# Half slots of an expert kernel: three instead of two of the four second-weight chunks in high and low parts

## Chip, core and metric

The kernel runs on one core of a Trainium2 chip. The metric is the device time of one execution in microseconds (us), lower being better. TensorE is called PE, VectorE DVE, ScalarE ACT, GpSimd POOL and SyncE (which issues the weight loads) SP, as in the profile.

## The reference

Three parts run one after the other: attention over 32 memories, a Fourier mixing with a dense feed-forward layer, and a routed expert layer. The change touches only the last one. Cut to what matters:

```
x: (4, 576, 512)   w_gate: (512, 8)   w1: (8, 512, 1024)   w2: (8, 1024, 512)
logits = x @ w_gate
for each token: e = its expert (argmax of its logits, or the expert of the token before it)
    p = softmax(logits)
    h = relu(x[b, s] @ w1[e])
    out[b, s] = p[e] * (h @ w2[e])
```

## The kernel before

**Slots.** The tokens of one expert are gathered in slots of up to 256. A slot loads eight weight chunks of 128x1024 fp32 (512 KB each): chunks 0 to 3 hold the expert's first weights, chunks 4 to 7 the second ones. Slots 0 and 1 are written out beside the end of the dense layer; slots 2 to 16 stand one after the other, each under a test on the number of slots, and each in two arms. The first arm is for a full slot. The second arm is for a half slot, one with at most 128 tokens (`narrow`, `turn` and `short_out`). In the profiled execution twelve slots run, and the half arm is taken in slots 3, 4 and 11, which the text calls A, B and C.

**Precision.** A product of fp32 quality is made in one of two ways. Either both factors are split in a high and a low part (type fp32r) and three fast matmuls are added (`products`, L1103 to L1105): high times high, high times low, low times high. Or both factors stay raw fp32 and one slow matmul is issued (L1253), which the trace records as two. Splitting a weight chunk is called a cut: ACT writes the high part (L1327) and DVE or POOL subtracts it from the raw chunk for the low part (L1329). In a half arm the low part of chunk 1 is made on POOL, those of the others on DVE.

**A half slot.** `narrow` makes the hidden values, 128 tokens by 256 for each of the first-weight chunks c = 0 to 3 (tile `pl`). `turn` applies the relu (L1173 on ACT, L1175 on DVE; tile `un`), transposes the result on PE (L1180), and brings it back from PSUM: for c below `SPLIT` as high part on ACT (L1192) and low part on DVE (L1194), for the others as one raw copy (L1185 on ACT or L1187 on DVE). `short_out` multiplies it by second-weight chunk 4 + c, two matmul steps for each c, and then ACT scales the sum (L1261) and POOL writes it out (L1266). The lines that read `SPLIT`:

```
1181            if c >= SPLIT:
1246                w = "cut" if c < SPLIT else "raw", j, 4 + c
1255            if c >= SPLIT and j + 1 < NS:
1448                     ("cut", "late")[arm]: [cuts(*[(j, c) for c in range(4, (8, 4 + SPLIT)[arm])]), cuts(*[(j + 1, c) for c in range(4)])]})
```

The last of these lines also shows that a slot's arm cuts chunks 0 to 3 of the next slot. Line 1255 reloads a chunk that was used raw after its last matmul; a chunk that is cut is reloaded after its cut.

**Order.** `weave` is a planner. Every task yields an engine, a length and what it depends on; the planner picks the step that can start first by its own estimates (`SLOTS`, `SLOT_PACE`) and writes the program in that order. On the chip every engine then runs its own instructions in the written order, and waits at the first one whose inputs are missing. SP does so too, with the weight loads.

Of the kernel before, what the change touches and what calls it, by code (L numbers as in the profile page):

```python
# [84 lines left out]
SLOT_PACE = {"T": 0.928, "V": 0.999, "S": 0.996, "G": 0.946, "D": 1.033}  # L85
LANES = 2
EARLY = 2
SPLIT = 2

FIELDS = ((("ident", 128), ("mask", 4), ("half", 1), ("big", 2)),  # L90
          (("s0", 18), ("tid", 18), ("desc", 8), ("iotaC", 256), ("ohR", 8), ("kR", 1), ("ones", 8), ("k256", 9),
# [86 lines left out]
def attention_fourier_experts_kernel(ctx, tc, qT, phi, kv, w1, w2, wg, wgc, wm, cs, cd, c1, c2, midx, out):  # L178
# [41 lines left out]
    def ended(*names):  # L220
        return [end.get(n, 0.0) for n in names]
# [879 lines left out]
    def products(ps, a, b, first, last):  # L1101

        T.matmul(ps, a[0], b[0], start=first, stop=False)  # L1103
        T.matmul(ps, a[0], b[1], start=False, stop=False)  # L1104
        T.matmul(ps, a[1], b[0], start=False, stop=last)  # L1105
# [58 lines left out]
    def turn(j):  # L1164
        for c in range(4):
# [13 lines left out]
            for x in range(2):  # L1179
                T.transpose(pt[:, 128 * x:128 * x + 128], hr[:, 128 * x:128 * x + 128], id_)  # L1180
            if c >= SPLIT:
                r = yield "SV", {"S": 0.35, "V": 0.42}, [r]
# [55 lines left out]
    def short_out(j):  # L1238
# [4 lines left out]
        for c in range(4):  # L1243
            for x in range(2):
                n = FFN + 8 * j + 2 * c + x
                w = "cut" if c < SPLIT else "raw", j, 4 + c
                yield lambda: ("hid", n) in end and w in end and ("yr", i - 3) in end
                r = yield "T", 0.69 if c < SPLIT else 0.86, ended(("hid", n), w, ("yr", i - 3))
                ts, q = slice(128 * x, 128 * x + 128), slice(512 * x, 512 * x + 512)
                if c < SPLIT:  # L1250
                    products(ps, (hid[n][0][:, ts], hid[n][1][:, ts]), (WH[4 + c][:, q], WL[4 + c][:, q]), c + x == 0, False)
                else:
                    T.matmul(ps, hid[n][:, ts], RAW[4 + c][:, q], start=False, stop=(c + x == 4))  # L1253
                end["used", j, 0, 2 * c + x] = r
            if c >= SPLIT and j + 1 < NS:
                end["raw", j + 1, 4 + c] = yield "D", 1.46, [r]
# [107 lines left out]
    def cuts(*jc):  # L1364
        for j, c in jc:
            yield lambda: j >= NS or all(x in end for x in used(j - 1, c))
            yield from cut(j, c)

    def gather(j):

        yield lambda: ("idx", min(j, 2)) in end and (j == 0 or ("x", NG + j - (2 if j > 2 else 1)) in end)
        yield lambda: j == 0 or ("land", j - 1, 1) in end
        x = gathered[j] = (gathered[j - 2] if j > 3 else
                           stg.tile([128, 1040], F32, name="stg").rearrange("p (t c) -> p t c", t=2))
        for h in range(2):
            end["land", j, h] = yield "G", 1.04, ended(("idx", min(j, 2)), ("ys", NG - 2 if j < 2 else NG - 1))
            G.indirect_dma_start(out=x[:, h], out_offset=None, in_=ys, in_offset=IO(ap=idx[:, h, j:j + 1], axis=0),
                                 bounds_check=N, oob_is_err=False)

    def tokens(j):  # L1380

        if j >= NS:
            return
        k = (NG + j) % 2
        if j < 3:
            yield from gather(j)
        yield lambda: ("land", j, 1) in end
        x = gathered[j]
        before = "first", (16 * NG - 17 if j == 0 else FFN - 1 if j == 1 else FFN + 8 * j - 9)
        yield lambda: before in end  # L1390
        for h in range(2):
            pt, r = yield from turned4(lambda kk: x[:, h, 128 * kk:128 * kk + 128], end["land", j, h] + (5.2 if j < 2 else 3.5))
            hs = slice(128 * h, 128 * h + 128)
            r = yield "S", 0.5, [r] + ended(before)
            S.copy(XH[k][:, :, hs], pt)
            r = yield "V", 0.62, [r]
            V.tensor_tensor(out=XL[k][:, :, hs], in0=pt, in1=f32(XH[k][:, :, hs]), op=ALU.subtract)
            free_pt(r)
            yield lambda: j < 2 or ("yr", 2 * (NG + j) - 3) in end
            yield "V", 0.07, []  # L1400
            j8 = sm_.tile([128, 8], F32, name="j8s")
            V.scalar_tensor_tensor(out=j8, in0=x[:, h, 512:520], scalar=1.0, in1=ohs[:, j] if j > 1 else ohP[:, j], op0=ALU.mult,
                                   op1=ALU.mult, accum_out=PV[k][:, h:h + 1])
        end["x", NG + j] = r
# [18 lines left out]
    with ExitStack() as es:  # L1423
        for j in range(2, NS):
# [13 lines left out]
            for arm in range(2):  # L1438
                with (cmp.Else() if arm else tc.If(half > 0, label=f"half{j}")) as cmp:  # L1439
                    if j + 1 in halves_of:  # L1440
                        tc.mark_branch_hint_location(f"half{j + 1}", halves_of[j + 1], [ET.PE])
                    if FIRST <= j + 1 < NS:
# [4 lines left out]
                    weave({**own, ("tokens", "rows")[arm]: [tokens(j + 1)], "ahead": [gather(j + 2)] if j + 2 < NS else [],  # L1447
                           ("cut", "late")[arm]: [cuts(*[(j, c) for c in range(4, (8, 4 + SPLIT)[arm])]), cuts(*[(j + 1, c) for c in range(4)])]})
                after = before if arm == 0 else full
# [31 lines left out]
```

## Time and profile before

| what | value |
|---|---|
| timed runs | 832.75, 836.06 and 835.94 us, median 835.94 us |
| the profiled execution | 832.19 us, of which the profile's span is 830.4 us |
| PE busy | 802.5 us, 97% of the span |
| DVE, ACT, POOL busy | 546.9, 307.1, 173.7 us |
| mean granted PE clock | 0.993 of full speed |

All times of instructions below are in us from the start of the span. An engine's instructions overlap a little (the next one starts before the end of the last), so what one costs in a row of its kind is the distance between starts. The matmuls' ends are modelled.

### The profile page before, as it was taken

Reading aid. Unit: us, or ns where it says so; the run is one execution under the profiler, and the core shown is the slowest. Engines: PE = TensorE matmul, PEld = TensorE weight load, DVE = VectorE, ACT = ScalarE, POOL = GpSimd, SP = SyncE. Lnnn points to the kernel's source line nnn. Section 1 sums busy time; section 2 is a strip of 40 time slices with the busy share of each in tenths; the row PEclk is TensorE's granted clock in tenths of the full one; section 3 lists DMA queues with packets and bytes.
Section 4 is the critical chain, followed back from the end, with each engine's and each line's share of the span. In section 5 each row is a group of like instructions: output and inputs, shape, how many; then the busy total and the mean of one; then the engine's idle time right before and its main releaser. Section 6 shows DMA issues by size and latency. Waiting matters only on the chain. (4 is left out here: it accounts for less than half of the span.)

```text
span 830.4 us, 14734 instructions
## 1 busy us (share of the span) xinstructions
PE 802.5 (97%) x5500; PEld 697.4 (84%) x5500; DVE 546.9 (66%) x1339; ACT 307.1 (37%) x590; POOL 173.7 (21%) x166
## 2 busy tenths in 40 slices
PE   7999999999999999999999999999999998999993
PEld 6676678888989989889998989889899886899881
DVE  2587766776476876868584766667786565765661
ACT  3465644765111111111111111144464445554441
POOL 0466553553000000000000000020222224121231
PEclk9999999999999999999999999999999999999997
DMA  9877345651310001010000000291786668866563
GB/s 350 339 253 284 117 133 178 218 178 52 130 37 27 26 26 30 24 52 1 27 26 26 26 27 1 83 348 54 258 278 225 208 205 325 301 219 248 199 212 131
DMA packets 35688, 122.09 MB, mean 147 GB/s; under 512 B 5204, under 2 KB 5460, under 8 KB 33802
## 3 DMA queue, kind: packets, MB, share of 16 engines
q1 hardware_dynamic: 30474, 103.76, 36.1%
q0 software_dynamic: 4688, 14.53, 5.1%
q10 hardware_dynamic: 432, 2.60, 0.9%
q8 instruction: 53, 0.87, 0.4%
q14 instruction: 41, 0.34, 0.1%
HBM read 106.10 MB, written 15.56 MB: 147 GB/s over the span
## 5 line engine op out<-in xcount | busy, mean ns | idle before, releaser
L1105 PE MATMUL pl<-xh,w1l 128*128 128x256 f32 x864 | 241.2, 279 | 0.0
L1105 PEld LDWEIGHTS pl<-xh,w1l 128*128 128x128 f32 x864 | 162.3, 188 | 0.0
L1103 PE MATMUL pl<-xh,w1h 128*128 128x256 f32 x576 | 162.3, 282 | 0.0
L1104 PE MATMUL pl<-xl,w1h 128*128 128x256 f32 x576 | 160.9, 279 | 0.0
L1144 ACT ACTIVATE hh<-pl 128x256 fp32r<-128x256 f32 x144 | 55.2, 384 | 281.5 <-PE pl L1105 266.9
L1329 DVE TENSOR_TENSOR w1l<-w1h,w2h 128x1024 fp32r<-128x1024 f32 x91 | 111.7, 1241 | 18.7 <-ACT w2h L1327 12.1
L1327 ACT CAST w2h<-w1h 128x1024 fp32r<-128x1024 f32 x94 | 96.9, 1047 | 49.6 <-issue 34.0
L1103 PEld LDWEIGHTS pl<-xh,w1h 128*128 128x128 f32 x576 | 108.2, 188 | 2.8
L1104 PEld LDWEIGHTS pl<-xl,w1h 128*128 128x128 f32 x576 | 108.1, 188 | 2.4
L1103 PE MATMUL y<-w2h,hh 128*128 128x512 f32 x272 | 108.9, 401 | 0.0
L1105 PE MATMUL y<-w2h,hl 128*128 128x512 f32 x272 | 106.9, 393 | 1.6 <-DVE hl L1146 1.6
L1104 PE MATMUL y<-w2l,hh 128*128 128x512 f32 x272 | 106.7, 392 | 0.5 <-POOL w2l L746 0.5
L840 DVE SCALAR_TENSOR_TENSOR jk<-stg,wgt 128x512 bf16<-128x512 f32 x144 | 99.0, 687 | 4.1 <-DMA wgt<-in_wg_dram 1.6
L1146 DVE SCALAR_TENSOR_TENSOR hl<-pl,hh 128x256 fp32r<-128x256 f32 x144 | 60.4, 421 | 56.1 <-ACT hh L1144 55.5
L1103 PE MATMUL pl<-xh,w2h 128*128 128x256 f32 x288 | 82.6, 287 | 0.0
L1104 PE MATMUL pl<-xl,w2h 128*128 128x256 f32 x288 | 80.8, 281 | 0.0
L349 POOL TENSOR_TENSOR rv<-rv,C 128x1 f32<-128x1 f32 x18 | 12.9, 715 | 269.9 <-DVE rv L347 258.3
L1105 PEld LDWEIGHTS y<-w2h,hl 128*128 128x128 f32 x272 | 51.1, 188 | 13.7 <-DVE hl L1146 2.4
L1103 PE MATMUL y<-w2h,w2l 128*128 128x512 f32 x156 | 62.4, 400 | 0.0
L1105 PE MATMUL y<-w2h,w2l 128*128 128x512 f32 x156 | 61.6, 395 | 0.0
L1104 PE MATMUL y<-w1l,w2l 128*128 128x512 f32 x156 | 61.4, 394 | 0.0
L1104 PEld LDWEIGHTS y<-w2l,hh 128*128 128x128 f32 x272 | 51.2, 188 | 8.9 <-POOL w2l L746 0.8
(249 smaller groups left out, 1350.6 us busy)
## 6 DMA issues: line engine op xcount, KB each, us to landing
w1h<-in_wm_dram SPq DMA_DIRECT2D x104, 512.0 KB
stg<-in_w_dram SPq DMA_DIRECT2D x21, 512.0 KB
kvt<-in_kv_dram SPq DMA_DIRECT2D x8, 1290.0 KB
wgt<-in_w_dram SPq DMA_DIRECT2D x11, 512.0 KB
ys<-stg SPq DMA_DIRECT2D x9, 520.0 KB
qt<-in_qT_dram SPq DMA_DIRECT2D x4, 1156.0 KB
ph<-in_phi_dram SPq DMA_DIRECT2D x8, 288.0 KB
u<-ut SPq DMA_DIRECT2D x12, 192.0 KB
```

What stands on the lines that cost most here:

```text
L349: G.tensor_tensor(out=rv, in0=rv, in1=c_("half"), op=ALU.pow)
L840: V.scalar_tensor_tensor(out=jk, in0=yt[:, t, 0:512], scalar=1.0, in1=wgt[:, e], op0=ALU.mult, op1=ALU.mult, accum_out=L[:, t, e:e + 1])
L1103: T.matmul(ps, a[0], b[0], start=first, stop=False)
L1104: T.matmul(ps, a[0], b[1], start=False, stop=False)
L1105: T.matmul(ps, a[1], b[0], start=False, stop=last)
L1144: S.activation(out=hh, in_=ps, func=AF.Relu)
L1146: V.scalar_tensor_tensor(out=hl, in0=ps, scalar=0.0, in1=f32(hh), op0=ALU.max, op1=ALU.subtract)
L1327: S.copy(WH[c], RAW[c])
L1329: E[mark["eng"]].tensor_tensor(out=WL[c], in0=RAW[c], in1=f32(WH[c]), op=ALU.subtract)
```

## The change

The constant `SPLIT` goes from 2 to 3. In every half arm, chunk 6 is therefore cut instead of used raw, and the hidden values for c = 2 come back from PSUM in a high and a low part.

```
@@ -85,7 +85,7 @@
 LANES = 2
 EARLY = 2
-SPLIT = 2
+SPLIT = 3
```

What this makes of the written order is shown by the half arm of slot 2; those of all other slots read alike but for the numbers of buffers. First DVE, from the low part of chunk 5 to the arm's end (`w1l5` is the low part of chunk 5, `w2l2` and `w2l4` hold the hidden values of c = 1 and c = 2):

```order
 L1329 TENSOR_TENSOR w1l5_105<-w1h5_6271,w2h5_1613 128x1024
 L1194 TENSOR_TENSOR w2l2_1240<-rl_1651,w2l2_1240 128x256
-L1187 COPY wgt_1628<-y2_1650 128x256
-L1329 TENSOR_TENSOR w1l2_102<-w1h2_6212,w2h2_1610 128x1024
+L1329 TENSOR_TENSOR w1l2_102<-w1h2_6212,w2h2_1610 128x1024
+L1194 TENSOR_TENSOR w2l4_1616<-y2_1650,w2l4_1616 128x256
+L1329 TENSOR_TENSOR w1l6_106<-w1h6_6307,w2h6_1614 128x1024
 L1329 TENSOR_TENSOR w1l3_103<-w1h3_6227,w2h3_1611 128x1024
 L1439 UNCONDITIONAL_BRANCH
```

The copy of the raw hidden values is gone; the low part of c = 2 and the low part of chunk 6 stand behind the low part of chunk 2, which belongs to the next slot.

Then ACT in the same stretch (`un` is the relu's output, `w2h6` the high part of chunk 6):

```order
 L1173 ACTIVATE un_7293<-pl_7247 128x256
 L1327 CAST w2h2_1610<-w1h2_6212 128x1024
+L1192 CAST w2l4_1616<-y2_1650 128x256
+L1327 CAST w2h6_1614<-w1h6_6307 128x1024
 L1173 ACTIVATE un_7293<-pl_7264 128x256
 L1327 CAST w2h3_1611<-w1h3_6227 128x1024
 L1185 COPY wgt_1628<-rl_1651 128x256
```

Two casts stand ahead of the relu of c = 3.

And PE, from the last product with chunk 5 to the raw matmuls with chunk 7 (`y1` is the output sum):

```order
 L1105 MATMUL y1_1649<-w2h5_1613,w2l2_1240 128x512
-L1253 MATMUL y1_1649<-w1h6_6307,wgt_1628 128x512 x2
+L1180 MATMUL rl_1651<-C_85,un_7293 128x128 x2
+L1103 MATMUL y1_1649<-w2h6_1614,w2l4_1616 128x512
+L1104 MATMUL y1_1649<-w1l6_106,w2l4_1616 128x512
+L1105 MATMUL y1_1649<-w2h6_1614,w2l4_1616 128x512
+L1103 MATMUL y1_1649<-w2h6_1614,w2l4_1616 128x512
+L1104 MATMUL y1_1649<-w1l6_106,w2l4_1616 128x512
+L1105 MATMUL y1_1649<-w2h6_1614,w2l4_1616 128x512
 L1253 MATMUL y1_1649<-w1h7_6392,wgt_1628 128x512 x2
```

Six products take the place of two raw matmuls, and the transposes of c = 3 (L1180), which stood three products earlier, come after all products with chunk 5. POOL's and SP's instructions keep their order; on SP the reload of chunk 6 now waits for DVE (its cut) instead of PE (its last raw matmul).

## Rows read from the trace of the kernel before

**Rows 1.** The page's part 1: busy time, share, instructions.

```profile
PE 802.5 (97%) x5500; PEld 697.4 (84%) x5500; DVE 546.9 (66%) x1339; ACT 307.1 (37%) x590; POOL 173.7 (21%) x166
```

**Rows 2.** Busy time by stretch, then clock, DMA share, GB/s: A, B, C.

```profile
678.18:691.91 13.73, 13.73 (x85) 11.14 (x84) 9.73 (x16) 7.86 (x13) 6.85 (x4) 1.00 0.75 259
691.91:708.17 16.26, 14.12 (x86) 11.04 (x84) 10.10 (x15) 9.30 (x15) 6.32 (x4) 1.00 0.82 292
802.36:816.10 13.74, 13.74 (x85) 11.01 (x83) 9.62 (x16) 7.85 (x13) 7.63 (x4) 1.00 0.73 240
```

**Rows 3.** Timeline of PE, the end of A: start, duration, instruction.

```profile
686.64 0.38 PE L1180 MATMUL y<-C,un 128*128 128x128 f32 x2
...
687.57 0.38 PE L1180 MATMUL rl<-C,un 128*128 128x128 f32 x2
...
688.25 0.40 PE L1105 MATMUL y<-w2h,w2l 128*128 128x512 f32 x1
688.48 3.60 PE L1253 MATMUL y<-w1h,wgt 128*128 128x512 f32 x8
691.91 0.60 PE L328 MATMUL pt<-C,stg 128*128 128x128 f32 x4
```

**Rows 4.** Waits of PE in 692 to 708.2: total, times, longest.

```profile
PE rl L1180 <- DVE un L1175: 1.6, 1, 1.6
```

**Rows 5.** Timeline of ACT, the end of A and a cast in B.

```profile
686.00 1.05 ACT L1327 CAST w2h<-w1h 128x1024 fp32r<-128x1024 f32 x1
686.94 0.40 ACT L1173 ACTIVATE un<-pl 128x256 f32<-128x256 f32 x1
687.21 1.06 ACT L1327 CAST w2h<-w1h 128x1024 fp32r<-128x1024 f32 x1
...
698.21 1.05 ACT L1327 CAST w2h<-w1h 128x1024 fp32r<-128x1024 f32 x1 [3.33 <-DMA w1h<-in_wm_dram]
```

**Rows 6.** Timeline of DVE in A, B and C: the cuts of chunks 2 and 3.

```profile
682.86 0.41 DVE L1194 TENSOR_TENSOR w2l<-y,w2l 128x256 fp32r<-128x256 f32 x1
683.20 0.41 DVE L1175 TENSOR_SCALAR un<-pl 128x256 f32<-128x256 f32 x1
...
687.40 2.53 DVE L1329 TENSOR_TENSOR w1l<-w1h,w2h 128x1024 fp32r<-128x1024 f32 x2
...
703.66 3.82 DVE L1329 TENSOR_TENSOR w1l<-w1h,w2h 128x1024 fp32r<-128x1024 f32 x2
...
811.58 2.48 DVE L1329 TENSOR_TENSOR w1l<-w1h,w2h 128x1024 fp32r<-128x1024 f32 x2
```

**Rows 7.** Line 1329 on DVE, same pairs: ns min/median/max, first and last start.

```profile
L1329 DVE TENSOR_TENSOR w1l<-w1h,w2h x2: 1209/1305/1401, 687.4 to 688.7; 128x1024 fp32r<-128x1024 f32 x2
...
L1329 DVE TENSOR_TENSOR w1l<-w1h,w2h x2: 1215/1948/2681, 703.7 to 706.3; 128x1024 fp32r<-128x1024 f32 x2
...
L1329 DVE TENSOR_TENSOR w1l<-w1h,w2h x2: 1212/1281/1350, 811.6 to 812.9; 128x1024 fp32r<-128x1024 f32 x2
```

**Rows 8.** Timeline of POOL: the cut of chunk 1 in A, B, C.

```profile
684.89 2.83 POOL L1329 TENSOR_TENSOR w1l<-w1h,w2h 128x1024 fp32r<-128x1024 f32 x1 [0.85 <-ACT w2h L1327]
...
701.99 3.27 POOL L1329 TENSOR_TENSOR w1l<-w1h,w2h 128x1024 fp32r<-128x1024 f32 x1 [4.15 <-ACT w2h L1327]
...
809.31 2.54 POOL L1329 TENSOR_TENSOR w1l<-w1h,w2h 128x1024 fp32r<-128x1024 f32 x1
```

**Rows 9.** Timeline of PE: the raw matmuls of B and of C.

```profile
704.74 3.59 PE L1253 MATMUL y<-w1h,wgt 128*128 128x512 f32 x8
...
812.66 3.60 PE L1253 MATMUL y<-w1h,wgt 128*128 128x512 f32 x8
```

**Rows 10.** Waits of PE in 708 to 760: total, times, longest.

```profile
PE pt L328 <- issue: 0.3, 1, 0.3
```

**Rows 11.** Busy time by stretch behind the last matmul, with the granted clock.

```profile
816.00:818.00 2.00, 0.25 (x1) 0.00 (x0) 0.00 (x0) 0.69 (x1) 0.74 (x1) 1.00 0.71 258
818.00:820.00 2.00, 0.00 (x0) 0.00 (x0) 0.00 (x0) 0.00 (x0) 0.29 (x1) 0.67 0.71 225
```

More of the change, by code (lines that the diff above doesn't have):

```diff
@@ L87 @@
 EARLY = 2
-SPLIT = 2
+SPLIT = 3
 FIELDS = ((("ident", 128), ("mask", 4), ("half", 1), ("big", 2)),
```

## The prediction

> **What bounds the kernel now.** I first read the busy times: PE is busy 97% of the span [rows 1], so what lengthens or shortens PE's stream moves the end. Then the stretches of the three half slots, since only their arms change: in A and C PE has no gap (13.73 of 13.73 and 13.74 of 13.74 us), in B it stands for 2.1 of 16.26 us [rows 2]. Of B's gap 1.6 us lie at one transpose that waits for DVE [rows 4], and this goes back to a load: ACT's cast of the next slot's chunk 0 waited 3.33 us for its DMA [rows 5], and DVE and PE came after it. So A and C are pure PE time, B is PE time with one late load in it.
>
> Last I laid the four engines' timelines of A's end side by side. What is to be seen there: PE reaches the raw matmuls with chunk 6 at 688.48 and finds everything ready [rows 3]. ACT and DVE at that moment are busy with cuts for the next slot, which nothing waits for yet [rows 5, 6]. The change puts work that PE needs at once into these two queues.
>
> **What is removed and added on PE.** In A the eight records of raw matmuls run from 688.48 to 691.91 [rows 3]; that is four matmuls of 3.43 / 4 = 0.857 us. A product of the split kind takes 688.48 - 688.25 = 0.23 us from start to start, three of them 0.69. Two raw matmuls become two triples in each half slot: 2 x (0.857 - 0.69) = 0.33 us less, 1.0 us in three slots. That is the whole direct gain.
>
> **What is added elsewhere.** In each half slot: one cast of a chunk on ACT (1.05 us [rows 5]), one low part of a chunk on DVE (1.21 us unhindered, the shorter of each pair in [rows 7]), one high part of 128x256 on ACT, and one low part of 128x256 on DVE in place of a copy of that size. In total the engines have room: DVE is busy 9.73 of 13.73 us in A, ACT 7.86 [rows 2]. The SP queue keeps its order and its bytes. What counts is the place in the order, since PE waits for the last of these.
>
> **When the new inputs are ready, in A.** ACT: the cast of chunk 2 starts at 686.00; the transposes of c = 2 end at 686.64 + 0.38 = 687.02 [rows 3]. So the high part of c = 2 goes at about 687.06, the cast of chunk 6 at about 687.3 and ends by 688.4, and the relu of c = 3, which ran at 686.94 [rows 5], runs only at about 688.3 to 688.7. PE's transposes of c = 3 stood at 687.57 [rows 3] and now wait until about 688.75. That is a gap of some 0.5 us, but it lies inside the longer one that follows, so it isn't counted.
>
> DVE: in the new order the low part of chunk 2 comes first, then that of c = 2, then that of chunk 6. Here a second thing matters. The low part of chunk 2 started at 687.40 and took 1.40 us, 2.68 us in B (from 703.66), 1.35 us in C (from 811.58), where its follower took 1.21 each time [rows 6, 7]. Each of the long ones began while POOL was still making the low part of chunk 1, which ended at 684.89 + 2.83 = 687.72, 701.99 + 3.27 = 705.26 and 809.31 + 2.54 = 811.85 [rows 8]. The ends on DVE are 688.80, 706.34 and 812.93: 1.08 us behind POOL's end in all three. DVE is thus held until POOL is through. The Trainium skill says the same as a rule (SBUF — State Buffer, section "SBUF: two separate sides"): the port pair that VectorE and GpSimd share is an exclusive lock, taken by a VectorE operation with two SBUF inputs against a GpSimd operation that reads SBUF, and the loser waits for the whole instruction. By that rule the held cut starts at POOL's end and takes its full time, 0.14 us later than measured in each slot, and the sum below would be 0.4 us larger; I keep the measured 1.08.
>
> The new order lets DVE start chunk 2 about 0.3 us earlier in A (at 687.08, when its cast is done, without the copy ahead of it), but still inside POOL's operation. So its end E stays where it is: 688.80, 706.34, 812.93. From E on: the next instruction starts 0.08 before E (687.40 + 2.53 - 1.21 = 688.72 for the second of the pair, against 688.80 [rows 6, 7]); the low part of c = 2 takes 0.34 from start to start (682.86 to 683.20 [rows 6]; one of its inputs lies in PSUM); the low part of chunk 6 takes 1.21. It ends at E - 0.08 + 0.34 + 1.21 = E + 1.47. I take 0.05 us for the signal to PE, about what lies between the transposes' end and the work that they released.
>
> PE's first product with chunk 6 needs only high parts and can run ahead. The second needs the low part of chunk 6. From there five products (5 x 0.23 = 1.15) and two raw matmuls with chunk 7 (2 x 0.857 = 1.71) remain. The slot's last matmul is through at E + 1.47 + 0.05 + 1.15 + 1.71 = E + 4.38.
>
> - A: 693.18 instead of 691.91, **+1.27**.
> - B: 710.72 instead of 704.74 + 3.43 = 708.17 [rows 9], **+2.55**. POOL was later here and E with it, so PE stands for over 2 us.
> - C: 817.31 instead of 812.66 + 3.43 = 816.09 [rows 9], **+1.22**.
>
> The 1.0 us saved is already inside these differences.
>
> **What is behind the waiting instructions.** On PE everything of the slot and the next slots stands behind the wait. In A and C PE had no gap that could take up a delay, and in the first 52 us behind B PE waited 0.3 us in all [rows 10]. On DVE the low part of chunk 3 moves behind that of chunk 6 and ends by about E + 2.6, before the slot's end. Its reader is the next slot, so this costs nothing; if that cover were gone it would cost at most its 1.21 us. The final scale and the output write stand behind the last matmul and move with it. On SP the reload of chunk 6 waits for its cut, which ends at 690.27 in A, where before it waited for the second raw matmul, at 688.48 + 1.71 = 690.19: the same. The reload of chunk 7 still waits for the slot's last matmuls, and the next slot's chunk 0 is issued behind it on the same queue. So in B the late load of chunk 0 stays as late relative to the slot's start as it was. I take nothing for it; from both sides it is bounded by 0 (nothing comes sooner) and by B's 1.6 us gap (chunk 6's earlier reload clears the way for all of it).
>
> **Sum.** 1.27 + 2.55 + 1.22 = 5.0 us more, 0.6%. The profiled execution had 832.19 us, so by its own time 837.2. The runs of before lie in two groups, 832.19 (the profiled one) and 832.75, and 835.94 and 836.06; the median of the timed three is in the upper one. The changed kernel's median can be in either: 837.2 or, 3.75 higher, 841.0. I name the mean of the four runs, 834.2, plus 5.0: **839.3 us**. For the likeliest case alone the range is 836 to 842.
>
> **Rivals.**
>
> 1. *DVE is not held by POOL.* Then the low part of chunk 2 runs from 687.08 to 688.29 in A, the slot ends at 688.29 + 4.38 = 692.67, and the cost is 0.76; three slots of this kind give 2.3 us: 834.5 by the profile's own time, 836.5 from the mean of runs. This is not slower by what can be told. For it: POOL's spans are rough. Against it: three of three operations end 1.08 behind POOL, with lengths from 1.35 to 2.68. The case in which B's late load comes 1.6 us sooner lies beside it: 5.0 - 1.6 = 3.4 us, 837.6. Together 0.2.
> 2. *The cut is hidden and PE gains.* This is the other side: PE never waits and the 1.0 us is kept, 831.2 by the own time, 833.2 from the mean; with all of B's gap taken up as well 2.6 us, still only 0.3%. It decides from the point where the low part of chunk 6 ends by 688.7, just behind the first product, in A. That needs it to start at about 687.5, and at that time chunk 2 occupies DVE until 688.80 and chunk 6's cast isn't done. Against it speaks the written order itself. 0.08.
> 3. *The clock falls in B.* PE would stand from about 705.4 to 707.9 there. Behind the last matmul the granted clock was still 1.00 in the stretch up to 818, 1.75 us after PE's work, and 0.67 in the mean of the next two us [rows 11], on its way from 2.4 to 1.2 GHz. A stand of 2.4 us lies between. If it falls, the 2.86 us of B's remaining matmuls take twice as long: 7.9 us in the sum, 840.1 to 843.9. 0.1.
> 4. *As worked out:* 0.62.
>
> **How the numbers follow.** About 0.5% (4.2 us) is what a measurement of this kernel can tell from no change, for its runs lie up to 3.9 us apart. The likeliest case stands just above this, so of its 0.62 I give three quarters to slower; nearly all of rival 3, a quarter of rival 1, and little of rival 2: 0.62 in all for slower. Faster by over 0.5% no mechanism here can give (2.6 us is its most); it is left to the runs' two groups, 0.04. The same holds 0.34. The range goes from rival 2 by the mean, 833.2, to rival 3 at the upper group, 843.9: 833.3 to 844.
>
> **What would show each step.** Right: in each of the three half slots PE waits for DVE's line 1329 at the second product with chunk 6, about 0.6 us in A and C and over 2 us in B; raw matmul records fall from 24 to 12; DVE's low part of chunk 2 still ends about 1.1 us behind POOL's; A and C are some 15.0 us long, B some 18.8. Wrong: no wait of PE at that line, or the low part of chunk 2 of 1.2 us although it begins during POOL's (rival 1); B's 1.6 us wait gone (the load comes sooner); a granted clock under 1.00 in B (rival 3). The forecast fails as a whole if PE can go on from c = 1 to c = 2 without standing, or if later slots have slack that this trace doesn't show.

## The result, and the profile after

| | before | changed |
|---|---|---|
| median of the runs, us | 834.59 (13 runs, 830.79 to 836.06) | 838.41 (13 runs, 836.43 to 841.68) |
| ratio, 95% interval | 1 | 1.0056 [1.0043, 1.0069] |
| profiled execution, us (span) | 832.19 (830.4) | 836.43 (834.7) |

The changed kernel is slower by 0.56%; on 834.6 us that is 4.7 us, with 3.6 to 5.8 as the interval's ends. (The two medians alone lie 3.82 us apart.) PE has six records more than in [rows 1] (18 more of the split products, 12 fewer of line 1253), and its busy share falls from 97% to 96%. Busy time by engine, from the page's first part:

```profile
PE 804.6 (96%) x5506; PEld 699.9 (84%) x5506; DVE 550.8 (66%) x1342; ACT 311.4 (37%) x596; POOL 174.5 (21%) x166
```

The same stretches as in [rows 2], half slots A, B and C of the changed kernel (busy us of PE, PEld, DVE, ACT, POOL, then granted clock, DMA share, GB/s):

```profile
677.58:692.69 15.11, 13.88 (x87) 11.44 (x86) 11.11 (x17) 9.18 (x15) 6.84 (x4) 1.00 0.75 264
692.69:711.55 18.86, 15.68 (x87) 12.64 (x86) 11.44 (x16) 10.51 (x17) 6.30 (x4) 0.91 0.72 252
805.78:820.83 15.05, 13.88 (x87) 11.28 (x85) 11.03 (x17) 9.17 (x15) 7.59 (x4) 1.00 0.74 249
```

A is 15.11 us where it was 13.73, B 18.86 where it was 16.26, C 15.05 where it was 13.74: +1.38, +2.60 and +1.31, together +5.29 us. Between B and C 94.23 us lie where 94.19 lay. So all of the loss is inside the three slots. The two profiled executions as wholes lie only 4.24 us apart, because in the changed kernel's A begins 0.60 us sooner and the part behind C is 0.48 us shorter. In A and C PE had no gap and now has one of 1.23 and 1.17 us. What PE waits for from 660 on (total, times, longest):

```profile
PE y L1104 <- DVE w1l L1329: 2.9, 3, 1.1
PE rl L1180 <- DVE un L1175: 1.8, 1, 1.8
```

Three waits for DVE's line 1329, one in each half slot; the second row is the late load of B that [rows 4] show too. The timeline of PE at the end of A, to be read beside [rows 3]:

```profile
688.12 0.44 PE L1180 MATMUL rl<-C,un 128*128 128x128 f32 x2 [0.30 <-ACT un L1173]
688.31 0.47 PE L1103 MATMUL y<-w2h,w2l 128*128 128x512 f32 x1
689.71 0.51 PE L1104 MATMUL y<-w1l,w2l 128*128 128x512 f32 x1 [0.93 <-DVE w1l L1329]
690.05 0.39 PE L1105 MATMUL y<-w2h,w2l 128*128 128x512 f32 x1
...
690.98 1.88 PE L1253 MATMUL y<-w1h,wgt 128*128 128x512 f32 x4
692.69 0.60 PE L328 MATMUL pt<-C,stg 128*128 128x128 f32 x4
```

The first product with chunk 6 runs at 688.31; it needs high parts only. The second reads the low part and starts at 689.71. DVE in A and B, the counterpart of [rows 6]:

```profile
683.61 1.21 DVE L1329 TENSOR_TENSOR w1l<-w1h,w2h 128x1024 fp32r<-128x1024 f32 x1
...
686.53 1.66 DVE L1329 TENSOR_TENSOR w1l<-w1h,w2h 128x1024 fp32r<-128x1024 f32 x1 [0.85 <-ACT w2h L1327]
688.11 0.41 DVE L1194 TENSOR_TENSOR w2l<-y,w2l 128x256 fp32r<-128x256 f32 x1
688.45 2.34 DVE L1329 TENSOR_TENSOR w1l<-w1h,w2h 128x1024 fp32r<-128x1024 f32 x2
...
704.15 2.89 DVE L1329 TENSOR_TENSOR w1l<-w1h,w2h 128x1024 fp32r<-128x1024 f32 x1
706.97 0.41 DVE L1194 TENSOR_TENSOR w2l<-y,w2l 128x256 fp32r<-128x256 f32 x1
707.30 2.34 DVE L1329 TENSOR_TENSOR w1l<-w1h,w2h 128x1024 fp32r<-128x1024 f32 x2
```

And POOL's cut of chunk 1 in A and B, the counterpart of [rows 8]:

```profile
684.29 2.81 POOL L1329 TENSOR_TENSOR w1l<-w1h,w2h 128x1024 fp32r<-128x1024 f32 x1 [0.84 <-ACT w2h L1327]
...
702.71 3.25 POOL L1329 TENSOR_TENSOR w1l<-w1h,w2h 128x1024 fp32r<-128x1024 f32 x1 [4.09 <-ACT w2h L1327]
```

In A POOL ends at 687.10 and DVE's cut of the next slot's chunk 2, begun at 686.53, at 688.19. In B it is 705.96 and 707.04: 1.09 and 1.08 us apart. (The first row of DVE is the cut of chunk 5, which was running when POOL's began; the account of the hold below comes back to it.) Only then come the hidden low part and chunk 6's low part, the first of the two records of the last row.

### The profile page after: what moved, and what is told of

Read it like the earlier page. It is cut to its first block, busy times and chain, and to the rows that moved or that the text cites. A ratio compares the mean times of both kernels' runs of the same rounds, so it can differ in the third digit from the quotient of the medians.

```text
span 834.7 us, 14756 instructions
## 1 busy us (share of the span) xinstructions
PE 804.6 (96%) x5506; PEld 699.9 (84%) x5506; DVE 550.8 (66%) x1342; ACT 311.4 (37%) x596; POOL 174.5 (21%) x166
## 5 line engine op out<-in xcount | busy, mean ns | idle before, releaser
L1329 DVE TENSOR_TENSOR w1l<-w1h,w2h 128x1024 fp32r<-128x1024 f32 x94 | 116.0, 1247 | 21.9 <-ACT w2h L1327 19.9
L1327 ACT CAST w2h<-w1h 128x1024 fp32r<-128x1024 f32 x97 | 99.9, 1046 | 43.0 <-issue 33.2
L1104 PE MATMUL y<-w1l,w2l 128*128 128x512 f32 x162 | 64.6, 398 | 2.9 <-DVE w1l L1329 2.9
L1103 PE MATMUL y<-w2h,w2l 128*128 128x512 f32 x162 | 65.4, 403 | 0.0
L1105 PE MATMUL y<-w2h,w2l 128*128 128x512 f32 x162 | 64.5, 398 | 0.0
```

Of the source, the lines that this page charges most:

```text
L1327: S.copy(WH[c], RAW[c])
L1329: E[mark["eng"]].tensor_tensor(out=WL[c], in0=RAW[c], in1=f32(WH[c]), op=ALU.subtract)
```

## The experiments

The theory: DVE's cut of the next slot's chunk 2 is held until POOL is through with chunk 1, chunk 6's low part stands behind it, and PE waits for that. The rivals: the added work on ACT and DVE costs by itself; ACT's high part of chunk 6 comes too late; the order costs without POOL; the load of B or the clock makes the difference.

The table has every kernel's profiled execution. A, B and the stretch between B and C run from one slot's first transpose (line 328) to the next one's; C runs to one distance between starts behind the start of its last matmul, some 0.16 us ahead of that matmul's modelled end. "Load wait" is PE's wait at B's first hidden transpose for what follows from the late load; the kernels 3 and 5 to 10 have a second one in B, 0.4 to 0.6 us for ACT's relu at the next hidden transpose, which the column leaves out. Ratios are to the kernel before on the same chip, from all comparable runs.

| kernel | A | B | load wait in B | between B and C | C | ratio, 95% interval |
|---|---|---|---|---|---|---|
| before | 13.73 | 16.26 | 1.6 | 94.19 | 13.74 | 1 |
| before, profiled again (11) | 13.73 | 18.54 | 2.39 | 94.31 | 13.73 | one execution |
| changed | 15.11 | 18.86 | 1.80 | 94.23 | 15.05 | 1.0056 [1.0043, 1.0069] |
| 1: no POOL cut | 14.49 | 17.63 | 2.50 | 96.44 | 14.43 | 1.003 [1.0018, 1.0042] |
| 2: cut made, not read | 13.79 | 18.08 | 2.37 | 94.97 | 13.67 | 1.0002 [0.9989, 1.0016] |
| 3: chunk 6 ahead of chunk 2 | 14.50 | 17.36 | 1.43 | 94.31 | 14.47 | 1.0019 [1.0007, 1.0031] |
| 4: four chunks split | 15.96 | 18.93 | 0.76 | 94.27 | 15.95 | 1.0077 [1.006, 1.0094] |
| 5: three, chunk 6 early, no POOL cut | 13.40 | 15.96 | 1.15 | 96.00 | 13.41 | 0.9988 [0.9974, 1.0002] |
| 6: four, 6 and 7 early, no POOL cut | 13.08 | 14.38 | none | 95.84 | 13.08 | 0.9953 [0.9936, 0.9971] |
| 7: two, no POOL cut | 13.72 | 16.86 | 1.43 | 96.15 | 13.65 | 1.0 [0.9983, 1.0017] |
| 8: as 5, with the POOL cut | 13.39 | 16.15 | 1.32 | 94.24 | 13.39 | 0.9963 [0.9948, 0.9979] |
| 9: as 6, with the POOL cut | 13.07 | 14.27 | none | 94.91 | 13.07 | 0.9936 [0.9916, 0.9956] |
| 10: as 5, with a memset on POOL | 13.22 | 16.16 | 1.34 | 94.91 | 13.24 | 0.9963 [0.9948, 0.9977] |
| 5, profiled again (12) | 13.39 | 15.61 | 0.81 | 96.50 | 13.35 | one execution |

A and C hold to 0.06 us from one execution to the next (the kernel before and kernel 5, each profiled twice; kernel 10's execution had everything on PE about 1.2% shorter, 92.98 us busy between B and C where kernel 5 had 94.12). B does not, and the runs 11 and 12 were made to see that.

**1. No cut on POOL.**

```diff
-                    mark["cut"] = ("V", "GV")[arm]
+                    mark["cut"] = ("V", "V")[arm]
```

> Edit: in half slots chunk 1 of the next slot gets its low part on DVE and no longer on POOL; all else as in the changed kernel, up to the order that follows from it (DVE: hidden low part, chunk 1, hidden low part, chunk 6, chunk 2, chunk 3). Theory (DVE is held by POOL at chunk 2's low part, and chunk 6 stands behind it): without an operation on POOL no low part on DVE is long, all are about 1.21 us; chunk 6 stands behind one cut of full length only. A is 0.75 us longer than in the kernel before, B 0.8, C 0.7, instead of 1.38, 2.60, 1.31: +2.2 us in all, a ratio of about 1.0027 to the kernel before and 0.997 to the changed one. Rival a (POOL plays no part, the new place in DVE's order alone costs): DVE has one more cut to make in each slot, so the same +5 us or more, B still +2.6. Rival b (ACT's chain of casts is what is late): PE waits no less at the second product with chunk 6, +5 us.

Measured: A +0.76 and C +0.69 to the kernel before, ratio 1.003. All low parts on DVE from 676 on, in ns, minimum, median, maximum:

```profile
L1329 DVE TENSOR_TENSOR w1l<-w1h,w2h x53: 1209/1219/1285, 678.9 to 819.0; 128x1024 fp32r<-128x1024 f32 x53
```

None is long any more. In the changed kernel the longest took 2893. B came out at +1.37 instead of +0.8, with a load wait 0.9 us longer than in the kernel before; PE's wait for the cut was 0.34 us there. With one cut more on DVE the kernel is faster than the changed one, so POOL's hold is about half of the loss (A and C fall from +1.38 and +1.31 to +0.76 and +0.69). The rest isn't DVE's queue alone. In A DVE comes to the low part of chunk 6 and stands for ACT's high part of it:

```profile
688.06 3.67 DVE L1329 TENSOR_TENSOR w1l<-w1h,w2h 128x1024 fp32r<-128x1024 f32 x3 [0.52 <-ACT w2h L1327]
```

It is 0.52 us in C too, and none in B. On ACT that cast stands behind the high part of the hidden values of c = 2, which waits for PE's transposes. So rival b, ACT's chain of casts, is true of what is left in A and C when the hold is gone.

**2. The cut made and not read.**

```diff
-SPLIT = 3
+SPLIT = 2
...
-                           ("cut", "late")[arm]: [cuts(*[(j, c) for c in range(4, (8, 4 + SPLIT)[arm])]), cuts(*[(j + 1, c) for c in range(4)])]})
+                           ("cut", "late")[arm]: [cuts(*[(j, c) for c in range(4, (8, 5 + SPLIT)[arm])]), cuts(*[(j + 1, c) for c in range(4)])]})
```

(The reload of chunk 6 stays behind PE's use of it, as in the kernel before.)

> Edit: PE reads chunk 6 uncut, as in the kernel before, but the half slots still make its high part on ACT and its low part on DVE, which nothing reads; hidden parts of c = 2 as in the kernel before. It holds the added work on ACT and DVE without PE's dependence on it. Theory (what costs is PE's wait for the low part of chunk 6): PE doesn't wait there, A and C are within 0.2 us of the kernel before, B within 0.5; ratio 1.000 (0.9985 to 1.001). Rival (the added work itself costs: the two queues are too full, or later casts and loads slip): +1.3 us in each of A and C and more in B, ratio about 1.005.

Measured: A +0.06, C -0.07, no wait for line 1329, ratio 1.0002. The added cast and cut cost nothing when PE doesn't read them, and the rival falls. B missed its bound (18.08, not within 0.5 of 16.26); run 11, where the unchanged kernel has 18.54, shows that this needn't be an effect of the edit.

**3. Chunk 6 ahead of the next slot's chunk 2.**

```diff
     def cuts(*jc):
         for j, c in jc:
             yield lambda: j >= NS or all(x in end for x in used(j - 1, c))
+            yield lambda: mark["full"] or not (c == 2) or ("cut", j - 1, 6) in end
```

> Edit: the changed kernel with the next slot's chunk 2 cut after this slot's chunk 6, on ACT and DVE; POOL keeps chunk 1. Theory (chunk 6 stands behind a cut that POOL holds): taken out of that place it waits for its own cast on ACT only, which ends at about 688.4 in A on the clock of the kernel before; A +0.75, B +1.2, C +0.75 to the kernel before, +2.7 us in all, ratio 1.003; the low part of chunk 2, now behind POOL's end, takes 1.21 us. Rival a (POOL holds whatever DVE starts next, so chunk 6 is held in place of chunk 2): A and C +1.0 to +1.3, B +2.5, ratio 1.005. Rival b (putting chunk 2 later delays the next slot's first products): PE waits at the start of the slots behind A, B and C, ratio above 1.005.

Measured: A +0.77, B +1.10, C +0.73, ratio 1.0019 (expected 1.003; the interval ends at 1.0031). POOL is still there, but what it would hold now starts when it is done or nearly so. What is left of the wait is ACT's cast of chunk 6, for which DVE stands 0.19 us in A:

```profile
687.48 0.41 DVE L1175 TENSOR_SCALAR un<-pl 128x256 f32<-128x256 f32 x1
688.09 3.50 DVE L1329 TENSOR_TENSOR w1l<-w1h,w2h 128x1024 fp32r<-128x1024 f32 x3 [0.19 <-ACT w2h L1327]
```

That A and C cost as much as in run 1 agrees with it: in both kernels ACT's cast ends DVE's wait. The sum of the slots is 2.60 against the first execution of the kernel before; the ratio says 1.6 us. Neither rival fits.

**4. Four chunks split, in the planner's own order.**

```diff
-SPLIT = 3
+SPLIT = 4
...
-                    products(ps, (hid[n][0][:, ts], hid[n][1][:, ts]), (WH[4 + c][:, q], WL[4 + c][:, q]), c + x == 0, False)
+                    products(ps, (hid[n][0][:, ts], hid[n][1][:, ts]), (WH[4 + c][:, q], WL[4 + c][:, q]), c + x == 0, c + x == 4)
```

> Edit: all four chunks of the second weights are split in half slots (the last product carries the end of the sum). Theory (each chunk added stands as one more low part of about 1.21 us, and the chunk behind it, in DVE's queue behind PE's need): PE waits at chunk 7 too; against the kernel before A +2.3, C +2.2, B +3.5 less up to 1.3 if chunk 7's earlier reload lets the next slot's chunk 0 come sooner: +7 to +8 us, ratio 1.008 to 1.0095. Rival a (PE gains 0.33 us with each chunk and the first wait covers the second): +4 us, ratio 1.005 or less. Rival b (B's late load goes away whole): B is shorter than in the changed kernel and PE's 1.8 us wait at the first transpose there is gone.

Measured: A +2.23, B +2.67, C +2.21, ratio 1.0077 (expected 1.008 to 1.0095); the load wait in B fell to 0.76 us, but didn't go away. PE's two waits in A, for chunk 6 and for chunk 7:

```profile
690.08 0.50 PE L1104 MATMUL y<-w1l,w2l 128*128 128x512 f32 x1 [0.68 <-DVE w1l L1329]
692.69 0.51 PE L1104 MATMUL y<-w1l,w2l 128*128 128x512 f32 x1 [0.95 <-DVE w1l L1329]
```

Each chunk that is added where the planner puts it is one more cut in front of PE. That the split as such doesn't cost, and costs only where it stands, the next two runs show.

**5. Three chunks, chunk 6 cut early.** Chunk 6 gets a task of its own in half slots, which is planned as soon as the first weights' products of c = 1 are.

```diff
-        r = yield "S", 1.0, ended(("raw", j, c), *used(j - 1, c))
+        if not mark["full"] and c in (6,):
+            yield lambda: ("first", FFN + 8 * j + 2) in end
+            r = yield "S", 1.0, ended(("first", FFN + 8 * j + 2))
+        else:
+            r = yield "S", 1.0, ended(("raw", j, c), *used(j - 1, c))
...
-                    mark["cut"] = ("V", "GV")[arm]
+                    mark["cut"] = ("V", "V")[arm]
...
-                           ("cut", "late")[arm]: [cuts(*[(j, c) for c in range(4, (8, 4 + SPLIT)[arm])]), cuts(*[(j + 1, c) for c in range(4)])]})
+                           ("cut", "late")[arm]: [cuts(*[(j, c) for c in range(4, (8, 6)[arm])]), *[cuts((j, c)) for c in range(6, (6, 4 + SPLIT)[arm])], cuts(*[(j + 1, c) for c in range(4)])]})
```

(The bias of "late" is 0.45 instead of 0.26.)

> Edit: the changed kernel (three chunks split), but in half slots chunk 6 is cut directly behind chunk 5, ahead of all cuts for the next slot, and the next slot's chunk 1 gets its low part on DVE. Theory (what costs is chunk 6's place behind held and full-length cuts of the next slot): PE no longer waits for the low part of chunk 6, and PE's direct gain of 0.33 us in each half slot shows: A and C 13.4 us (0.3 to 0.4 less than in the kernel before), B 0.36 less apart from its late load, whose wait has been 0.8 to 2.5 us in the runs so far; ratio 0.9987 (0.997 to 1.000). Rival a (the split itself costs, through the added cast and cut): A and C stay above 14 us, ratio 1.003 or more. Rival b (the next slot's chunks 1 to 3 are cut too late now): PE waits in the first products of the slots behind A and B, ratio above 1.001.

Measured: A -0.33, C -0.33, no wait of PE for a low part, ratio 0.9988, whose interval holds 1. The slots show the direct gain of 0.33 us that the prediction worked out from [rows 3] and that the wait hid. Chunk 6 now stands early both on ACT and on DVE; no run parts the two.

**6. Four chunks, 6 and 7 cut early.** As 5 with SPLIT = 4, chunk 7 planned behind the first weights' products of c = 3, the last product ending the sum as in 4.

```diff
+        if not mark["full"] and c > 5:
+            n = FFN + 8 * j + (2 if c == 6 else 6)
+            yield lambda: ("first", n) in end
+            r = yield "S", 1.0, ended(("first", n))
```

> Edit: as the run with chunk 6 cut early, with all four chunks split and chunk 7 cut directly behind chunk 6. Theory: PE waits for no cut of its own slot and gains 0.33 us four times instead of twice as much as two: A and C 13.0 to 13.1 us (0.7 less than in the kernel before); in B chunk 7's reload no longer waits for the slot's last matmuls, the next slot's chunk 0 is loaded sooner behind it, and PE's wait at the first transpose shrinks below 0.5 us: B 14 to 14.5. In all -3 to -4 us, ratio 0.995 to 0.9965. Rival a (the load is late for want of bandwidth, not for its place in the queue): B's wait stays at 0.8 to 2.5 us, ratio 0.9975. Rival b (the next slot's cuts come too late): PE waits behind A and B, ratio 1.000 or more.

Measured: ratio 0.9953, and in A, B and C (columns as above):

```profile
678.08:691.16 13.08, 13.08 (x90) 11.89 (x89) 11.48 (x18) 10.49 (x17) 4.04 (x3) 1.00 0.72 227
691.16:705.54 14.38, 13.52 (x89) 11.70 (x88) 11.71 (x19) 11.63 (x19) 3.41 (x3) 1.00 0.92 320
801.38:814.46 13.08, 13.07 (x88) 11.75 (x88) 10.40 (x17) 10.49 (x17) 4.14 (x3) 1.00 0.67 209
```

PE has no gap in A and C. In B PE no longer waits at the first hidden transpose; 0.62 us are left at the second, for ACT's relu behind the casts. ACT's cast of the next slot's chunk 0 starts at

```profile
696.29 1.05 ACT L1332 CAST w2h<-w1h 128x1024 fp32r<-128x1024 f32 x1 [2.45 <-DMA w1h<-in_wm_dram]
```

which is 5.13 us into the slot; in the kernel before it was 698.21 - 691.91 = 6.30 [rows 5]. Chunk 7's reload no longer waits for the slot's last matmuls, and the load behind it on the same queue comes sooner. Kernel 9 shows the same (697.11 - 692.10 = 5.01 us), and kernel 4 has 5.11; in all eleven executions whose chunk 7 is used raw it is 5.8 to 7.0.

**7. Two chunks, no POOL cut.**

```diff
-SPLIT = 3
+SPLIT = 2
...
-                    mark["cut"] = ("V", "GV")[arm]
+                    mark["cut"] = ("V", "V")[arm]
```

(Bias 0.45 as in 5 and 6.)

> Edit: the kernel before (two chunks split) with the next slot's chunk 1 cut on DVE in half slots and the order that the last two kernels have otherwise (bias of the next slot's cuts 0.45 instead of 0.26). It tells how much of their change is due to this alone. Theory (in the kernel before nothing that PE needs in the slot stands behind DVE's cuts): A and C 13.7 us, as before, B as before within the scatter of its late load; ratio 1.000 (0.9985 to 1.0015). Rival (taking chunk 1 from POOL, or the later cuts of the next slot, is itself what gains or costs): A and C differ by more than 0.3 us or PE waits in the slots behind.

Measured: A 13.72, C 13.65, ratio 1.0. So what 5 and 6 gain isn't gained by taking POOL out or by the bias.

**8. Chunk 6 early, chunk 1 on POOL.**

```diff
-        end["cut", j, c] = r = yield mark["cut"], {"G": 2.46, "V": 1.2}, [r]
+        end["cut", j, c] = r = yield ("G" if c == 1 and not mark["full"] else mark["cut"]), {"G": 2.46, "V": 1.2}, [r]
```

> Edit: chunk 6 cut early as in the first kernel of this call, but the next slot's chunk 1 on POOL as in the changed kernel. It tells the place in the queue from POOL's part. Theory (the place decides: chunk 6's low part starts on DVE before POOL has its input, so nothing that PE needs stands behind a held cut): as with chunk 1 on DVE, A and C 13.4 us, ratio 0.9987 (0.997 to 1.000); only cuts for the next slot may be long on DVE. Rival (POOL holds chunk 6's cut or the hidden low part behind it wherever they stand): a DVE operation of 2 us or more stands ahead of PE's second product with chunk 6, A and C 14.5 us or more, ratio 1.003 or more.

Measured: A and C 13.39, ratio 0.9963, which is below the expected range. In the profiled executions 1.76 of the 2.48 us by which this kernel is shorter than kernel 5 lie between B and C, where kernel 5 has the wait ahead of C that is left open below. DVE at the end of A:

```profile
686.33 1.22 DVE L1333 TENSOR_TENSOR w1l<-w1h,w2h 128x1024 fp32r<-128x1024 f32 x1
687.60 0.42 DVE L1194 TENSOR_TENSOR w2l<-y,w2l 128x256 fp32r<-128x256 f32 x1
688.79 0.42 DVE L1187 COPY wgt<-rl 128x256 f32<-128x256 f32 x1 [0.77 <-PE rl L1180]
689.13 1.80 DVE L1333 TENSOR_TENSOR w1l<-w1h,w2h 128x1024 fp32r<-128x1024 f32 x1
```

and POOL:

```profile
687.26 2.59 POOL L1333 TENSOR_TENSOR w1l<-w1h,w2h 128x1024 fp32r<-128x1024 f32 x1 [3.09 <-ACT w2h L1331]
```

Chunk 6's cut (686.33) begins before POOL's and takes 1.22 us. The cut that is held, from 689.13 to 690.93, 1.08 us behind POOL's end at 689.85, is the next slot's chunk 2, and PE waits for nothing behind it. POOL's hold is still there; in A, B and C it costs nothing, since no operand that PE needs there stands behind it.

**9. Four early, chunk 1 on POOL.** Kernel 6 with the edit of 8.

> Edit: all four chunks split, chunks 6 and 7 cut early as in the run with four early chunks, but the next slot's chunk 1 gets its low part on POOL. The four kernels so far without that POOL operation had one more wait of PE, 1.4 to 1.8 us at C's first transpose for nothing that the profile shows, the six with it had none. Theory: both gains add up; A and C 13.05 us, B 14.4 (its late load gone), the 94.2 us between B and C as in the kernel before; ratio 0.9953 less 1.6 us, 0.9934 (0.992 to 0.995). Rival a (POOL holds a cut that PE needs when two chunks are cut early): A and C 14 us or more, ratio above 0.998. Rival b (the wait ahead of C comes with the order, not with POOL): it is there again, ratio 0.995 to 0.997.

Measured: ratio 0.9936, A and C 13.07, B 14.27. Between B and C 94.91 us lie, 0.7 more than expected: in the slot behind B PE stands 0.99 us at a transpose (line 328) for DVE, which has three cuts to make first, the first of them held to 2.53 us; kernel 6, without POOL's cut, has 0.33 us at that place. So here the hold does reach PE, one slot later. This is the fastest kernel of the study, at 0.9936 / 1.0056 = 0.988 of the changed one; its interval overlaps with that of 6, so that POOL's cut is better than DVE's here isn't shown.

**10. A memset on POOL.** Kernel 5 with one unread memset in each half slot:

```diff
+        if c == 1 and not mark["full"]:
+            G.memset(sm_.tile([128, 8], F32, name="j8p"), 0.0)
```

> Edit: three chunks split, chunk 6 cut early, chunk 1 on DVE, and a memset of 128x8 on POOL in each half slot, whose result nothing reads. It asks whether the wait at C's first transpose (1.57 us in the run with chunk 6 early and no POOL cut, none in the one with the POOL cut) goes with any instruction of POOL in the half slot. If so: C's first transpose doesn't wait, ratio about 0.997. If it goes with the low part of chunk 1 itself, its length or its place: the wait is 1.4 to 1.8 us again, ratio about 0.9988. In both cases A and C are 13.4 us, since nothing of the slot waits for a cut.

Measured: the wait at C's first transpose is there, 1.6 us, so it doesn't go away with any instruction of POOL. Yet the ratio is 0.9963, as for the kernel without that wait. A and C are 13.22 and 13.24, not 13.4, as everything on PE was shorter in this execution.

**11 and 12. Two kernels profiled again, unchanged.**

> The kernel before, unchanged, profiled once more. It tells how far two executions of one kernel lie apart in the places that the comparison uses. If PE's wait for B's late load and the wait at C's first transpose belong to a kernel: 1.6 us again in B (16.3 us), no wait ahead of C, 94.2 us between B and C. If they belong to the execution: the wait in B anywhere between 0.8 and 2.5 us as in the runs so far, perhaps 1.4 to 1.8 us ahead of C, and the time accordingly above the 832.19 us of the first profile, near the median of the runs (834.6). A and C, which contain no load that is late, should be 13.7 us in either case.

> The kernel with three chunks split, chunk 6 early and no POOL cut, profiled once more. If the wait at C's first transpose belongs to the kernel it is 1.4 to 1.8 us again; if it belongs to the execution it may be gone, and the stretch between B and C is then 94.2 us instead of 96.0. A and C 13.4 us in either case.

Measured for the kernel before: 834.42 us, A and C 13.73, but B 18.54 instead of 16.26. All 2.23 us between its two executions (834.42 - 832.19) are in B. PE there:

```profile
702.02 0.44 PE L1180 MATMUL rl<-C,un 128*128 128x128 f32 x2 [2.39 <-DVE un L1175]
```

and the stretches of B, of 702.5 to 706.5 in it, and of 704 to 708, which overlaps it:

```profile
691.99:710.53 18.54, 15.66 (x86) 12.21 (x85) 8.90 (x15) 9.29 (x15) 6.31 (x4) 0.91 0.73 256
702.50:706.50 4.00, 4.00 (x14) 3.09 (x13) 2.81 (x7) 2.90 (x6) 3.27 (x1) 0.57 0.87 309
...
704.00:708.00 4.00, 4.00 (x15) 2.80 (x15) 2.81 (x4) 1.77 (x4) 2.04 (x1) 0.76 0.54 175
```

The load came later (ACT's cast of the next slot's chunk 0 started 7.01 us into the slot instead of 6.30) and PE waited 2.39 us instead of 1.6; in the 4 us behind that wait the granted clock was 0.57 in the mean. That is 0.8 us of waiting and about 1.5 us of slower matmuls. Kernel 5, again: the wait ahead of C was 0.89 us instead of 1.57, so its size belongs to the execution.

## Why the prediction was right, step by step

The forecast was 839.3 us; measured were 838.41. The sum was +5.0 us; the slots show +5.29 between the two profiled executions, the runs 4.7 (3.6 to 5.8). The mechanism came true as worked out: PE waits for the low part of chunk 6, which stands behind a cut that POOL holds. That the total came so close is in part luck, as the paragraphs on B and on the base show.

**The hold on DVE.** As forecast, the end E of chunk 2's low part lies 1.08 to 1.09 us behind POOL's in A, B and C. So does the held cut in every execution that has this overlap: 21 of 21 pairs in the kernel before (both executions), the changed one, 2, 4, 8 and 9. The rule of the Trainium skill (SBUF — State Buffer, section "SBUF: two separate sides"), that the instruction which comes second waits for the whole of the other's, agrees in kind with runs 1 and 8: without POOL's operation no low part is long, and where DVE's comes first it takes its 1.22 us. By the rule the held one would end a full 1.21 us behind; measured is 0.13 less. One case in kernel 3 hints that POOL is through some 0.1 us before its row ends: in B a cut that began on DVE 0.04 us before the end of POOL's took 1.22 us and wasn't held. Rival 1 (DVE not held, 2.3 us) gives the size that run 1 measured, 1.003 or 2.5 us, but by another path: the rival left PE waiting for DVE alone, and in run 1 DVE stood for ACT in A and C. The prediction had put ACT's chain aside as shorter, which it is only while the hold lasts.

What the prediction didn't see is that the hold goes both ways. It took POOL's end as given. But POOL's cut of chunk 1 itself begins while DVE is busy with another cut (chunk 5 in the changed kernel's A: 683.61 + 1.21 = 684.82, against POOL's start at 684.29), and it ends 2.24 to 2.31 us behind the end of that DVE cut in 23 of 23 cases, with lengths from 2.49 to 3.30 us; the one POOL cut that began with DVE free (kernel 3, B) took 2.39. So in A E follows from DVE's own cut of chunk 5: 684.82 + 2.29 + 1.08 = 688.19. DVE's instructions with at most one input in SBUF (L1187, L1194) ran inside POOL's cut in their usual 0.42 us.

**The step from E to the slot's end.** In A E is 688.19, PE's second product with chunk 6 starts at 689.71 and the slot ends at 692.69: E + 1.52 and E + 4.50, where E + 1.52 and E + 4.38 were worked out. The missing 0.12 us is the first product behind the wait: 690.05 - 689.71 = 0.34 us from start to start instead of the 0.23 that the sum took from an undisturbed stretch. The same is in B and C (+4.51, +4.52), so this one term was 0.3 to 0.4 us too small in all. The wait of PE at that product was named as about 0.6 us in A and C; it was 0.93 and 0.86. The 0.6 doesn't follow from the prediction's own times: from the transposes at 688.75 to the second product at 690.32 are 1.57 us, of which the transposes and the first product take 0.66 (688.12 to 688.31, and 0.47, in the rows above), so about 0.9 was to be named. The sum didn't use it.

**The direct gain** of 0.33 us a slot was right, and runs 5, 6, 8 and 9 show it bare: one chunk more gives -0.33 to -0.35 us in A and C, two more -0.65 to -0.67.

**B.** Its length was foreseen to 0.05 us (18.86 against 18.81). This is luck in part: E came 14.35 us into the slot instead of 14.43, and that made up for most of the 0.13 us that the step from E lacked. How PE spends B was not foreseen: "PE stands for over 2 us" was wrong, it stood 1.15. The clock had fallen before, behind the load wait of 1.80 us, which was not one of the rivals' places. PE's rows from there:

```profile
701.95 0.44 PE L1180 MATMUL rl<-C,un 128*128 128x128 f32 x2 [1.80 <-DVE un L1175]
...
703.46 0.63 PE L1104 MATMUL y<-w1l,w2l 128*128 128x512 f32 x1
703.88 0.63 PE L1105 MATMUL y<-w2h,w2l 128*128 128x512 f32 x1
...
708.56 0.50 PE L1104 MATMUL y<-w1l,w2l 128*128 128x512 f32 x1 [1.15 <-DVE w1l L1329]
```

Products follow at 0.42 to 0.43 us instead of 0.23, and the granted clock of this stretch is half:

```profile
702.70:706.00 3.30, 3.30 (x10) 2.54 (x9) 3.20 (x3) 2.44 (x5) 3.25 (x1) 0.51 0.93 310
```

It cost nothing that the rows show, because PE still came to chunk 6's second product before its low part was done. Rival 3 (a fall in B) thus came true in place and time other than named, and without its price.

**What the sum was made against.** The weakest step is the base of B's term: "710.72 instead of ... 708.17". It takes B of one execution, whose load was early. Against the second execution of the kernel before B is only 0.32 longer, and the sum 3.0 instead of 5.3. The 4.7 us of the runs lie between the two; how much a later load adds to the changed kernel wasn't profiled. So the closeness of 5.0 to the runs' 4.7 rests in part on which execution happened to be profiled. The prediction saw four runs of the kernel before, up to 3.9 us apart, took them for two groups and averaged over them; the thirteen runs now on record spread from 830.79 to 836.06 without a gap between two groups, so that step had no ground. B's load and the clock behind it explain the 2.2 us between the two executions; whether it explains the other runs is not shown.

**What stays open.** PE's wait at C's first transpose, for which the profile shows no cause, is in the kernels 1, 5, 6, 7 and 10, which have no cut on POOL in half slots (0.9 to 1.8 us in six executions), and in none of the eight executions with one. A memset in its place didn't remove it. It hardly shows in the ratios: kernel 10 has it and comes out like kernel 8, which doesn't.

## What to carry to other kernels

Work moved to an engine that is a third idle can still be late: look up what stands in that engine's queue at the moment when the waiting engine needs the operand, and whether an operation there is held by another engine. Where an operand passes two engines, as here ACT and DVE, look at both queues: with the hold gone, the other one set the time. The same split cost 0.56% where the planner's order put its cut behind the next slot's, and gained 0.5% to 0.6% when all four chunks were split and cut ahead of them. Before a stretch's length is used as a base, profile the unchanged kernel twice: A and C repeated to 0.01 us, B differed by 2.3.

## What the runs showed of the hardware

- A DVE cut (two inputs in SBUF) that began during POOL's cut ended 1.08 to 1.09 us behind it in 21 of 21 cases, with lengths from 1.32 to 2.94 us; unhindered it takes 1.21.
- POOL's cut that began during a DVE cut ended 2.24 to 2.31 us behind that one in 23 of 23 cases; begun with DVE free it took 2.39 (one case). The profile shows both holds as longer instructions and not as waits.
- The granted clock fell to half around PE's waits of 1.80 (changed kernel), 2.37 (kernel 2) and 2.39 us (kernel before, again), and around the 2.25 us for which PE waited for chunk 6 in B of kernel 4. It fell between 0.4 us before the wait's end and 0.8 us behind it, for 3 to 4 us. It didn't fall at 1.6 (kernel before) or 2.50 (kernel 1, granted clock 1.00 through all of B). The length of the wait alone doesn't decide it.
- At full clock the first product behind a wait for a low part was followed by the next after 0.33 to 0.34 us (13 of 13 waits in the changed kernel and kernels 1, 3 and 4), where products otherwise follow at 0.23.
